# Staging of weight chunks: two steps ahead and in four buffers, with the low words converted in one piece

## The chip, the cores and the metric

The kernel runs on one NeuronCore of one Trainium2 chip. The metric is the device time of one execution in microseconds (us). Three runs of the kernel before took 1066.29, 1068.15 and 1068.39 us; the median is 1068.15.

## The reference, cut to what matters

Windowed attention with global tokens, then a feed-forward block. Batch 8, 8 heads, 512 local and 32 global tokens, head size 64; 4608 tokens in all, model width 512, inner width 2048.

```
s_ll = where(|i - j| <= 32, scale * q_l @ k_l^T, -1e9);  s_lg = scale * q_l @ k_g^T
out_l = softmax([s_lg, s_ll]) @ [v_g, v_l]
out_g = softmax(scale * q_g @ [k_g, k_l]^T) @ [v_g, v_l]
x = concat(out_g, out_l), heads side by side          # 4608 x 512
h = x @ w_in;  g = s * relu(h)**2 + b;  out = g @ w_out
```

The two weight matrices reach the kernel as 64-bit floats (they are passed as 64-bit words, two 32-bit words each). The kernel itself turns every value into a pair of 32-bit numbers, a rounded high part and a rest, with which TensorE later multiplies.

## The kernel before

The work is a sequence of steps j = 0, 1, 2, ... (the loop at the end of the function). Step j holds one attention slot (128 slots: batch, half of the 512 tokens, head) and, from step 10 on, one piece m = j - 10 of the feed-forward block (FFN; 136 pieces: 17 token tiles by 8 pairs of weight rows). Slot names carry their number: `sm9` is the softmax tile of slot 9, `ps_s9` its scores, `ps_t9` its transposed weights, `ps_o9` the products with the values, `rq9` and `rk9` its loaded queries and keys, `rv9` its values. FFN piece m has `ps_h` (first product), `r` (relu and square), `g` and the accumulators `acc`.

Slots 0 to 15 work with full 32-bit multiplication, slots from 16 on with split numbers: `kq` holds the split keys and queries of two slots, `vs` split values, `vsg` and `pg` what the global tokens need. `xs` (two buffers) holds the split tokens of a tile: tile 0 is complete after slot 7, tile 1 after slot 15.

The weights come in 16 chunks. Chunk k is 128 rows of `w_in` and 128 of `w_out`, two loads of 512 KB into a staging tile `wst`. Its decoding (`weight_words`) goes back and forth between ScalarE (ACT) and VectorE (DVE):

- ACT L155: the low words, converted (`wup`), 512 at a time, in the two buffers of `vs`
- ACT L157: the high words, scaled, over the low words
- DVE L158: shift and mask; DVE L162: add `wup`; DVE L163: put the sign back
- ACT L168: the high part into `w_all`; DVE L169: the rest into `w_all`

FFN piece m multiplies with chunks 2m and 2m + 1 (for m = 0 to 7; later tiles use the same weights). Chunks 0 and 1 are staged in the two `xs` buffers, chunks 2 to 15 in the two buffers of `kq`. Step j issues the loads of chunk j and then its decoding, so that a load must wait until the chunk two before it has been decoded.

The order of instructions on each engine isn't the program's order: the tile framework lists the instructions by a simulated time line, with priorities from the program's order. Each engine then works through its list in order; SyncE's queue (SP) issues nearly all loads, in order too, and waits where a buffer isn't free. For the first ten slots some matmuls on a constant tile (`warm`, L104) keep TensorE (PE) busy.

Of the kernel before, what the change touches and what calls it, by code (L numbers as in the profile page):

```python
# [11 lines left out]
F32R = mybir.dt.float32r  # L12
BF16 = mybir.dt.bfloat16
I32 = mybir.dt.int32
U32 = mybir.dt.uint32
U16 = mybir.dt.uint16
I16 = mybir.dt.int16
AF = mybir.ActivationFunctionType
ALU = mybir.AluOpType
# [3 lines left out]
P = 128  # L23
HALF = 256
# [7 lines left out]
NC = 416  # L32
# [19 lines left out]
WARM_FIRST = 28  # L52
WARM_HEAD = 4

SPOTS = ["xs"] * 2 + ["kq"] * 14
CHUNKS_AT = {j: 1 for j in range(16)}
BY_HALVES = 2
NORM_ACT = lambda j: j < NF
X_ACT = lambda j: j >= 8
# [2 lines left out]
G_LD = (0, 2)  # L62
G_PV = (1, 3)
GL_POOL = lambda m: False
XS_GAP, G_GAP = 0, 0
K_POOL = lambda j: j % 2


def f32(ap):
    return ap.bitcast(F32)  # L70
# [3 lines left out]
def window_attention_then_ffn(ctx: ExitStack, tc: tile.TileContext, qd, qg, kw, vw, vg, qz, qgz, vz, w_in, w_out, sv, bv, out):  # L74
    nc = tc.nc
    scale = 1.0 / math.sqrt(D)

    ops = ctx.enter_context(tc.tile_pool(name="ops", bufs=1))
# [1 line left out]
    masks = {first: ops.tile([P, 192 if first else 224], BF16, name=f"mask{int(first)}") for first in (True,)}  # L80
    w_all = ops.tile([P, 2, 16, 2, DM], F32R, name="w_all")
    gap = ops.tile([P, 240], F32, name="gap")
    for tag, n, bufs in (("vs", 512, 2), ("qgs", 512, 1), ("u", 256, 1), ("xs", 2048, 2), ("sm", NC, 2), ("pt", 2 * NC, 2), ("space", 16, 1), ("g", 1024, 2)):
        ops.tile([P, n], F32R, tag=tag, name=f"first_{tag}", bufs=bufs)
    const = ctx.enter_context(tc.tile_pool(name="const", bufs=1))
    sb = ctx.enter_context(tc.tile_pool(name="sb", bufs=2))
# [22 lines left out]
    for first, parts in ((True, ((32, 192, 0),)), (False, ((0, 160, 0), (192, 224, 32)))):  # L109
# [3 lines left out]
        for c0, c1, skip in parts:  # L113
            for sign, base in ((1, c0 - skip), (-1, 64 - c0 + skip)):
                nc.gpsimd.affine_select(
                    out=mask[:, c0:c1], in_=mask[:, c0:c1], pattern=[[sign, c1 - c0]], compare_op=ALU.is_ge,
# [11 lines left out]
    unread = sb.tile([P, 1], F32, tag="gm", name="unread", bufs=1)  # L128
    nc.scalar.activation(out=unread, in_=warm[:, 0:1], func=AF.Exp)

    def split_tile(tag, name, shape, gap):
        n = math.prod(shape)
        whole = ops.tile([P, n + gap], F32R, tag=tag, name=name, bufs=2)
        return whole[:, 0:n].rearrange("p (a b c) -> p a b c", a=shape[0], b=shape[1])

    def weight_chunk(k):
        st = ops.tile([P, 2048], I32, tag=SPOTS[k], name=f"wst{k}", bufs=2)
        n = 2 if k < BY_HALVES else 1
        sources = (w_in[k], w_out[k * P:(k + 1) * P, :])
        for i in range(2):  # L140
            queue = nc.scalar if k == 0 else nc.sync
            queue.dma_start(st[:, 1024 * i:1024 * (i + 1)], sources[i])
        for i in range(n):
            c = 1024 // n
            weight_words(k, st[:, 2 * c * i:2 * c * (i + 1)], slice(c * i, c * (i + 1)))

    def weight_words(k, st, at):
        words = st.rearrange("p (n w) -> p n w", w=2)
        low, high = words[:, :, 0], words[:, :, 1]
        n = at.stop - at.start  # L150
        parts = [slice(c, c + 512) for c in range(0, n, 512)]
        ups = []
        for h in parts:
            up = ops.tile([P, 512], I32, tag="vs", name=f"wup{k}_{at.start + h.start}", bufs=2)
            nc.scalar.activation(out=up, in_=low[:, h].bitcast(U32), func=AF.Copy, scale=2.0**-29)  # L155
            ups.append(up)
        nc.scalar.activation(out=low.bitcast(F32), in_=high.bitcast(F32), func=AF.Copy, scale=2.0**-112)  # L157
        nc.vector.tensor_scalar(  # L158
            out=low, in0=low, scalar1=3, scalar2=0x7FFFFFFF, op0=ALU.logical_shift_left, op1=ALU.bitwise_and,
        )  # L160
        for h, up in zip(parts, ups):
            nc.vector.tensor_tensor(out=low[:, h], in0=low[:, h], in1=up, op=ALU.add)  # L162
        nc.vector.scalar_tensor_tensor(  # L163
            out=high, in0=high, scalar=-2**31, in1=low, op0=ALU.bitwise_and, op1=ALU.bitwise_or,
        )
        m = high.bitcast(F32)
        hi, lo = (w_all[:, i, k].rearrange("p w c -> p (w c)")[:, at] for i in range(2))
        nc.scalar.copy(out=hi, in_=m)  # L168
        nc.vector.tensor_sub(out=lo, in0=m, in1=f32(hi))  # L169
# [190 lines left out]
    def qg_load(b):  # L360
        rqg = sb.tile([P, H * SG], F32, tag="xr", name=f"rqg{b}", bufs=1)
        nc.sync.dma_start(rqg, qgz[0] if b == 0 else qg[b])
        st_["rqg", b] = rqg

    def qg_load32(b):
        n = min(NF - 16 * b, H) * SG
        rqg = ops.tile([P, n], F32, tag="u", name=f"rqw{b}", bufs=1)
        nc.sync.dma_start(rqg, qgz[b, :, 0:n])
        st_["rqg", b] = rqg
# [129 lines left out]
    xs_ = {}  # L499

    def x_split(t):
        xs = split_tile("xs", f"xs{t}", [2, 4, HALF], XS_GAP)
        x = xcur.pop(t)
        for i in range(2):
            v = slice(2 * i, 2 * i + 2)
            nc.scalar.copy(out=xs[:, 0, v, :], in_=x[:, v, :])
            nc.vector.tensor_sub(out=xs[:, 1, v, :], in0=x[:, v, :], in1=f32(xs[:, 0, v, :]))
        xs_[t] = xs

    def xg_split(t):  # L510
        xs = split_tile("xs", f"xs{t}", [2, 4, HALF], XS_GAP)
        for i in range(2):
            xr = sb.tile([P, DM], F32, tag="r", name=f"xgr{i}", bufs=2)
            nc.sync.dma_start(xr, xg_d[i * P:(i + 1) * P, :])
            p_t = ps.tile([P, 4, P], F32, tag="t", name=f"ps_xg{i}")
            for c in range(4):
                nc.tensor.transpose(out=p_t[:, c, :], in_=xr[:, c * P:(c + 1) * P], identity=ident)
            q = slice(i * P, (i + 1) * P)
            nc.scalar.copy(out=xs[:, 0, :, q], in_=p_t)
            nc.vector.tensor_sub(out=xs[:, 1, :, q], in0=p_t, in1=f32(xs[:, 0, :, q]))  # L520
        xs_[t] = xs
# [3 lines left out]
    def ffn_in(m):  # L525
        t, pr = m // 8, m % 8
        xs = xs_[t]
        p_h = ps.tile([P, 2, HALF], F32, tag="h", name=f"ps_h{m}", bufs=2)
        for k in range(2):
            f = 2 * pr + k  # L530
            n = 0
            for c in range(4):
                for a, e in ((0, 0), (0, 1), (1, 0)):
                    nc.tensor.matmul(  # L534
                        p_h[:, k], lhsT=wi[:, a, f, c], rhs=xs[:, e, c, :],
                        start=(n == 0), stop=(n == 11),
                    )
                    n += 1
        r = sb.tile([P, 2, HALF], F32, tag="r", name=f"r{m}", bufs=2)
        nc.scalar.activation(out=r, in_=p_h, func=AF.Relu)  # L540
        nc.vector.scalar_tensor_tensor(out=r, in0=p_h, scalar=s_t, in1=r, op0=ALU.mult, op1=ALU.mult)  # L541
        g = split_tile("g", f"g{m}", [2, 2, HALF], G_GAP)
        if GL_POOL(m):
            nc.vector.tensor_scalar_add(r, r, b_t)
            nc.scalar.copy(out=g[:, 0], in_=r)
            nc.gpsimd.tensor_sub(out=g[:, 1], in0=r, in1=f32(g[:, 0]))
        else:
            nc.scalar.activation(out=g[:, 0], in_=r, func=AF.Identity, bias=b_t)  # L548
            nc.vector.scalar_tensor_tensor(  # L549
                out=g[:, 1], in0=r, scalar=b_t, in1=f32(g[:, 0]), op0=ALU.add, op1=ALU.subtract,  # L550
            )
        gs_[m] = g
# [35 lines left out]
    for b in range(B):  # L588
        for g in range(2):
# [4 lines left out]
            for i in range(2):  # L594
                h = 4 * g + 2 * i
# [19 lines left out]
    piece, last = 0, None  # L615
# [3 lines left out]
    for j in range(NM + LAG + 2):  # L619
        sp(j + 1)  # L620
        ld(j + 2)
        vl(j)
        for _ in range(CHUNKS_AT.get(j, 0)):
            weight_chunk(piece)
            piece += 1
        if j < NS:
            b1 = j // 16 + 1
            if j == 14 and NF > 16:
                qg_load32(1)
            elif j % 16 == 14 and b1 < B:  # L630
                qg_load(b1)
            sc(j)
            if j == NF - 1 and NF % 16:
                if NF > 16:
                    qg_load(j // 16)
                qg_split(j // 16)
            if j % 16 == 15 and NF <= j + 1 < NS:
                qg_split(b1)
        if j in early:
            early.pop(j)()  # L640
        m = j - LAG if LAG <= j < NM + LAG else None
        if m is not None:
            ffn_in(m)
            if m == 8 * 15 + 7:
                xg_split(16)
        tr(j - 1)
        transposes_and_pv(j - 1, j - 2)
        vsp(j - 1)
        for fn in extra.pop(j, []):
            fn()  # L650
        pvs(j - 2)
        vl32(j)
        if j in SPLIT_AT:
            x_split(SPLIT_AT[j])
        if last is not None:
            ffn_out(last)
        last = m
        if j in late:
            late.pop(j)()
# [79 lines left out]
```

## Time and profile before

| | us |
|---|---|
| median of three runs | 1068.15 |
| profiled execution | 1067.84 |
| its span | 1066.1 |
| PE busy / DVE / ACT / POOL in the span | 1024.1 / 814.6 / 725.6 / 315.0 |
| warm matmuls L104 | 18.6 |

PE is busy for 96% of the span, but not evenly: of 40 slices those after the sixth all show 9 (90% or more) except the last, and the first six show 9, 7, 8, 9, 7 and 7. "Busy" includes time at the lower clock and the warm matmuls. DMA is busiest in the same first slices.

### The profile page before, as it was taken

Reading aid. Unit: us, or ns where it says so; the run is one execution under the profiler, and the core shown is the slowest. Engines: PE = TensorE matmul, PEld = TensorE weight load, DVE = VectorE, ACT = ScalarE, POOL = GpSimd, SP = SyncE. Lnnn points to the kernel's source line nnn. Section 1 sums busy time; section 2 is a strip of 40 time slices with the busy share of each in tenths; the row PEclk is TensorE's granted clock in tenths of the full one; section 3 lists DMA queues with packets and bytes.
Section 4 is the critical chain, followed back from the end, with each engine's and each line's share of the span. In section 5 each row is a group of like instructions: output and inputs, shape, how many; then the busy total and the mean of one; then the engine's idle time right before and its main releaser. Section 6 shows DMA issues by size and latency. Waiting matters only on the chain.

```text
span 1066.1 us, 20403 instructions
## 1 busy us (share of the span) xinstructions
PE 1024.1 (96%) x7100; PEld 925.0 (87%) x7100; DVE 814.6 (76%) x2069; ACT 725.6 (68%) x1821; POOL 315.0 (30%) x365
## 2 busy tenths in 40 slices
PE   9789779999999999999999999999999999999996
PEld 4578669999999998999999999999999999999895
DVE  5878785887879968897879887997889787964321
ACT  6897685776768767786778676876678677743221
POOL 1000151432434423442344242432344234301000
PEclk9899789999999999999999999999999999999998
DMA  6755341221213222221323121322222122201000
GB/s 258 234 174 192 121 129 45 87 91 34 91 59 107 61 67 64 80 89 41 95 66 99 51 90 58 98 72 67 64 80 90 42 94 65 73 1 47 22 20 20
DMA packets 63535, 88.89 MB, mean 83 GB/s; under 512 B 7624, under 2 KB 48584, under 8 KB 63432
## 3 DMA queue, kind: packets, MB, share of 16 engines
q1 hardware_dynamic: 63144, 86.54, 25.9%
q8 instruction: 56, 0.92, 0.3%
q10 hardware_dynamic: 288, 1.05, 0.3%
q14 instruction: 47, 0.39, 0.1%
HBM read 78.12 MB, written 9.44 MB: 82 GB/s over the span
## 4 chain that ended last, share of the span: by engine, by line
PE 78%; DVE 8%; ACT 6%; DMA 5%; issue 1%; POOL 0%; SPq 0%; ACTq 0%; DVEq 0%; POOLq 0%
PE acc L566 32%; PE ps_h L534 30%; PE ps_t L326 4%; PE ps_o L412 4%; PE ps_s L385 4%; DMA wst<-in_w_in 2%; DMA wst<-in_w_out 2%; PE ps_og L486 2%; ACT sm L232 1%; DVE sm L242 1%; PE ps_g L391 1%; DVE w_all L169 1%; PE ps_tg L464 1%; DVE wst L162 1%; ACT wst L157 1%
## 5 line engine op out<-in xcount | busy, mean ns | idle before, releaser
L534 PE MATMUL ps_h<-xs,w_all 128*128 128x256 f32 x3264 | 441.0, 282 | 10.9 <-DVE w_all L169 3.9
L534 PEld LDWEIGHTS ps_h<-xs,w_all 128*128 128x128 f32 x3264 | 410.4, 190 | 22.9 <-DVE w_all L169 4.6
L566 PE MATMUL acc<-w_all,g 128*128 128x512 f32 x1632 | 426.1, 398 | 0.6 <-ACT g L548 0.3
L566 PEld LDWEIGHTS acc<-w_all,g 128*128 128x128 f32 x1632 | 291.5, 189 | 51.8 <-ACT g L548 1.1
L206 POOL TENSOR_TENSOR kq<-rq,kq 128x256 fp32r<-128x256 f32 x112 | 98.2, 877 | 235.8 <-ACT kq L205 219.8
L214 POOL TENSOR_TENSOR vs<-rv,vs 128x256 fp32r<-128x256 f32 x112 | 85.8, 766 | 261.4 <-ACT vs L213 248.5
L541 DVE SCALAR_TENSOR_TENSOR r<-ps_h,s_t,r 128x512 f32<-128x512 f32 x136 | 101.4, 746 | 61.2 <-ACT r L540 60.8
L540 ACT ACTIVATE r<-ps_h 128x512 f32<-128x512 f32 x136 | 81.1, 597 | 83.1 <-PE ps_h L534 75.5
L232 ACT ACTIVATE sm<-sm,nm 128x224 f32<-128x224 f32 (+1 forms) x256 | 118.5, 466 | 20.8 <-DVE nm L226 19.6
L549 DVE SCALAR_TENSOR_TENSOR g<-r,b_t,g 128x512 fp32r<-128x512 f32 x136 | 107.3, 789 | 32.6 <-ACT g L548 28.4
L548 ACT ACTIVATE g<-r,b_t 128x512 fp32r<-128x512 f32 x136 | 98.8, 727 | 45.8 <-DVE r L541 44.3
L226 DVE CUSTOM_DVE_ANT_0 sm<-ps_s,mask 128x224 f32<-128x224 f32 (+1 forms) x256 | 85.3, 368 | 23.4 <-PE ps_t L326 12.6
L326 PE MATMUL ps_t<-ident,sm 128*128 128x128 f32 x512 | 95.5, 280 | 5.1 <-ACT sm L240 5.0
L478 POOL TENSOR_TENSOR vsg<-rvg,vsg 128x320 fp32r<-128x320 f32 x64 | 57.1, 911 | 94.3 <-ACT vsg L477 94.2
L412 PE MATMUL ps_o<-pt,vs 128*128 128x256 f32 x448 | 83.6, 282 | 0.8 <-DVE u L424 0.8
L242 DVE TENSOR_SCALAR sm<-sm,nm 128x192 f32<-128x192 f32 (+1 forms) x224 | 81.8, 405 | 3.3
L385 PE MATMUL ps_s<-kq 128*128 128x192 f32 (+1 forms) x448 | 78.0, 280 | 4.3 <-ACT u L423 2.7
L385 PEld LDWEIGHTS ps_s<-kq 128*128 128x128 f32 x448 | 68.9, 193 | 10.6 <-ACT u L423 2.8
L395 ACT COPY tg<-ps_g 32x256 f32<-32x256 f32 (+1 forms) x112 | 42.2, 377 | 46.4 <-PE ps_g L391 44.0
L204 POOL TENSOR_TENSOR kq<-rk,kq 64x416 fp32r<-64x416 f32 x56 | 66.8, 1193 | 21.6 <-ACT kq L203 18.2
L401 ACT CAST pt<-ps_t 128x416 fp32r<-128x416 f32 x112 | 57.3, 511 | 22.9 <-PE ps_t L326 22.2
L412 PEld LDWEIGHTS ps_o<-pt,vs 128*128 128x128 f32 x448 | 67.1, 191 | 3.6 <-DVE u L424 1.0
(73 smaller groups left out, 1240.2 us busy)
## 6 DMA issues: line engine op xcount, KB each, us to landing
rq<-in_qd SPq DMA_DIRECT2D x112, 128.0 KB, 2.0
rv<-in_vw SPq DMA_DIRECT2D x112, 128.0 KB, 2.0
rk<-in_kw SPq DMA_DIRECT2D x64, 208.0 KB, 2.4
rvg<-in_vg SPq DMA_DIRECT2D x32, 320.0 KB, 2.9
out<-o SPq DMA_DIRECT2D x34, 256.0 KB, 2.2
wst<-in_w_in SPq DMA_DIRECT2D x15, 512.0 KB, 4.4
wst<-in_w_out SPq DMA_DIRECT2D x15, 512.0 KB, 5.5
rv<-in_vz SPq DMA_DIRECT2D x16, 256.0 KB, 3.0
```

The lines of the kernel that those rows point to most:

```text
L206: nc.gpsimd.tensor_sub(out=qs[:, 1, :], in0=rq, in1=f32(qs[:, 0, :]))
L214: nc.gpsimd.tensor_sub(out=vs[:, :, 1, :], in0=rv4, in1=f32(vs[:, :, 0, :]))
L232: nc.scalar.activation(out=p, in_=p, func=AF.Exp, bias=nm[:, blk:blk + 1], scale=-1.0, accum_out=ss[:, blk:blk + 1],)
L242: nc.vector.tensor_scalar(out=p, in0=p, scalar1=ss[:, blk:blk + 1], scalar2=1.0, op0=ALU.mult, op1=ALU.mult,)
L326: nc.tensor.transpose(out=p_t[:, at:at + P], in_=sm[:, c0:c0 + P], identity=ident)
L385: nc.tensor.matmul(p_s[:, cols], lhsT=qs[:, a, blk * P:(blk + 1) * P], rhs=ks[:, cols], start=(a == 0), stop=(a == 1),)
L412: nc.tensor.matmul(p_o[:, blk, :, q0:q0 + n], lhsT=vs[:, 2 * blk + c], rhs=pt[:, :, o], start=(c == 1), stop=(c == 0),)
L534: nc.tensor.matmul(p_h[:, k], lhsT=wi[:, a, f, c], rhs=xs[:, e, c, :], start=(n == 0), stop=(n == 11),)
L541: nc.vector.scalar_tensor_tensor(out=r, in0=p_h, scalar=s_t, in1=r, op0=ALU.mult, op1=ALU.mult)
L548: nc.scalar.activation(out=g[:, 0], in_=r, func=AF.Identity, bias=b_t)
L549: nc.vector.scalar_tensor_tensor(out=g[:, 1], in0=r, scalar=b_t, in1=f32(g[:, 0]), op0=ALU.add, op1=ALU.subtract,)
L566: nc.tensor.matmul(oacc[t][i], lhsT=g[:, a, k, i * P:(i + 1) * P], rhs=wo[:, e, f, :], start=(pr == 0 and n == 0), stop=(pr == 7 and n == 5),)
```

## The change

The staging tiles of the weights get four buffers in place of two. The two buffers of `xs` become two tags of one buffer each, `xs0` and `xs1` (even and odd token tiles), so that each can be named: chunk 4 is staged in `xs0` too, and chunks 5, 8, 11 and 14 in `xs1`; the rest stay in `kq`. The loads become a function of their own, `weight_load`, that step j calls for chunk j + 2 (steps 0 and 1 call it for four chunks), while `weight_chunk` decodes chunk j at step j as before. The low words of a chunk from 2 on are converted in one instruction of 1024 in place of two of 512, and added in one; `wup` moves from the `vs` buffers to those of `vsg` (even chunks) and `pg` (odd chunks). XS_GAP and G_GAP, which were 0, go.

```
-SPOTS = ["xs"] * 2 + ["kq"] * 14
-CHUNKS_AT = {j: 1 for j in range(16)}
+SPOTS = ["xs0", "xs1", "kq", "kq"] * 2 + ["xs1", "kq", "kq"] * 2 + ["xs1", "kq"]
+LOADS_AT = {0: (0, 1), 1: (2, 3), **{j: (j + 2,) for j in range(2, 14)}}
...
-    def weight_chunk(k):
-        st = ops.tile([P, 2048], I32, tag=SPOTS[k], name=f"wst{k}", bufs=2)
-        n = 2 if k < BY_HALVES else 1
+    staged = {}
+
+    def weight_load(k):
+        st = ops.tile([P, 2048], I32, tag=SPOTS[k], name=f"wst{k}", bufs=1 + (SPOTS[k] == "kq"))
+        staged[k] = st
         sources = (w_in[k], w_out[k * P:(k + 1) * P, :])
         for i in range(2):
             queue = nc.scalar if k == 0 else nc.sync
             queue.dma_start(st[:, 1024 * i:1024 * (i + 1)], sources[i])
+
+    def weight_chunk(k):
+        st = staged.pop(k)
+        n = 2 if k < BY_HALVES else 1
...
-        parts = [slice(c, c + 512) for c in range(0, n, 512)]
-        ups = []
-        for h in parts:
-            up = ops.tile([P, 512], I32, tag="vs", name=f"wup{k}_{at.start + h.start}", bufs=2)
-            nc.scalar.activation(out=up, in_=low[:, h].bitcast(U32), func=AF.Copy, scale=2.0**-29)
-            ups.append(up)
+        pool, tag = ((ops, "vsg"), (sb, "pg"))[(k + at.start // 512) % 2]
+        up = pool.tile([P, n], I32, tag=tag, name=f"wup{k}_{at.start}", bufs=1)
+        nc.scalar.activation(out=up, in_=low.bitcast(U32), func=AF.Copy, scale=2.0**-29)
...
-        for h, up in zip(parts, ups):
-            nc.vector.tensor_tensor(out=low[:, h], in0=low[:, h], in1=up, op=ALU.add)
+        nc.vector.tensor_tensor(out=low, in0=low, in1=up, op=ALU.add)
...
-        for _ in range(CHUNKS_AT.get(j, 0)):
-            weight_chunk(piece)
+        for k in LOADS_AT.get(j, ()):
+            weight_load(k)
+        if j < 16:
+            weight_chunk(j)
             piece += 1
```

How the order of instructions moves is shown at three places. The first is SP's queue of loads, around those of chunk 8 (`wst8`), in the kernel before (a name's last number is a buffer's):

```order
L276 DMA rq13_725<-in_qz 128x256
L270 DMA rk14_821<-in_kw 128x416
L281 DMA rv10_723<-in_vz 128x512
L362 DMA rqg1_1022<-in_qg 128x256
L276 DMA rq14_823<-in_qz 128x256
L281 DMA rv11_805<-in_vz 128x512
L142 DMA wst8_553<-in_w_in 128x1024
L142 DMA wst8_553<-in_w_out 128x1024
L142 DMA wst9_595<-in_w_in 128x1024
L142 DMA wst9_595<-in_w_out 128x1024
```

The same place of SP's queue in the changed kernel:

```order
L271 DMA rk8_444<-in_kw 128x416
L277 DMA rq8_446<-in_qz 128x256
L143 DMA wst8_448<-in_w_in 128x1024
L143 DMA wst8_448<-in_w_out 128x1024
L282 DMA rv5_442<-in_vz 128x512
L282 DMA rv6_483<-in_vz 128x512
L143 DMA wst9_487<-in_w_in 128x1024
L143 DMA wst9_487<-in_w_out 128x1024
L277 DMA rq9_485<-in_qz 128x256
```

The loads of chunk 8 stood behind the queries of slot 14 and now stand behind those of slot 8.

The second place is ACT's list just ahead of the relu of FFN piece 3 (`r3`), in the kernel before:

```order
L155 ACTIVATE wup9_0_598<-wst9_595 128x512
L155 ACTIVATE wup9_512_600<-wst9_595 128x512
L548 ACTIVATE g2_880<-r2_877,b_t_87 128x512
L157 ACTIVATE wst9_595<-wst9_595 128x1024
L168 CAST w_all_60<-wst8_553 128x1024
L240 ACTIVATE sm13_924<-sm13_924,nm13_925 128x224
L240 ACTIVATE sm13_924<-sm13_924,nm13_925 128x192
L540 ACTIVATE r3_960<-ps_h3_935 128x512
```

ACT's list ahead of the same relu in the changed kernel:

```order
L158 ACTIVATE wup15_0_1060<-wst15_879 128x1024
L549 ACTIVATE g2_854<-r2_851,b_t_88 128x512
L233 ACTIVATE sm13_895,nm13_896<-sm13_895,nm13_896 128x224
L233 ACTIVATE sm13_895,nm13_896<-sm13_895,nm13_896 128x192
L241 ACTIVATE sm12_816<-sm12_816,nm12_817 128x224
L241 ACTIVATE sm12_816<-sm12_816,nm12_817 128x192
L204 CAST kq16_1053<-rk16_975 64x416
L204 CAST kq16_1053<-rk16_975 64x416
L159 ACTIVATE wst15_879<-wst15_879 128x1024
L478 CAST vsg0_0_1227<-rvg0_0_1225 128x5x64
L478 CAST vsg0_0_1227<-rvg0_0_1225 128x5x64
L541 ACTIVATE r3_931<-ps_h3_906 128x512
```

At the same relu the decoding stood at chunk 9 and now stands at chunk 15, while attention stands at slot 13 in both.

The third place is PE's list just ahead of the first product of FFN piece 9 (`ps_h9`), in the kernel before:

```order
L391 MATMUL ps_g20_1644<-kq20_1518,qgs1_1125 64x256
L385 MATMUL ps_s21_1732<-kq20_1518 128x192 x2
L385 MATMUL ps_s21_1732<-kq20_1518 128x224 x2
L326 MATMUL ps_t19_1694<-ident_58,sm19_1534 128x128 x4
L412 MATMUL ps_o18_1691<-pt18_1592,vs18_1595 128x256
L412 MATMUL ps_o18_1691<-pt18_1592,vs18_1595 128x2x64
L412 MATMUL ps_o18_1691<-pt18_1592,vs18_1595 128x256
L412 MATMUL ps_o18_1691<-pt18_1592,vs18_1595 128x2x96
L385 MATMUL ps_s22_1844<-kq22_1723 128x192 x2
L385 MATMUL ps_s22_1844<-kq22_1723 128x224 x2
L534 MATMUL ps_h9_1547<-xs1_1387,w_all_60 128x256 x24
```

PE's list ahead of the same product in the changed kernel:

```order
L413 MATMUL ps_o16_1424<-pt16_1313,vs16_1316 128x2x64
L327 MATMUL ps_t17_1427<-ident_58,sm17_1264 128x128 x2
L413 MATMUL ps_o16_1424<-pt16_1313,vs16_1316 128x256
L413 MATMUL ps_o16_1424<-pt16_1313,vs16_1316 128x2x96
L327 MATMUL ps_t17_1427<-ident_58,sm17_1264 128x128 x2
L567 MATMUL acc0_1_785<-w_all_60,g7_1305 128x512 x5
L392 MATMUL ps_g18_1378<-kq18_1248,qgs1_1084 64x256
L567 MATMUL acc0_1_785<-w_all_60,g7_1305 128x512
L386 MATMUL ps_s19_1486<-kq18_1248 128x192 x2
L386 MATMUL ps_s19_1486<-kq18_1248 128x224 x2
L535 MATMUL ps_h9_1506<-xst1_1346,w_all_60 128x256 x24
```

At this product attention had come to the scores of slot 22 and now comes to those of slot 19; the second product (`acc`) of piece 7 now stands ahead of it.

## Rows read from the trace of the kernel before

**Rows 1.** Two stretches: start:end, length, busy us and count by engine, granted clock, DMA.
```profile
0.00:160.00 160.00, 130.40 (x727) 101.81 (x728) 121.99 (x281) 126.23 (x282) 24.68 (x36) 0.89 0.54 184
160.00:1066.10 906.10, 893.66 (x6374) 823.17 (x6374) 692.64 (x1789) 599.34 (x1541) 290.30 (x329) 1.00 0.22 66
```
**Rows 2.** Chain that ended last, first 160 us: shares by line.
```profile
by line: DMA wst<-in_w_in 16.5%; DMA wst<-in_w_out 11.1%; DVE w_all L169 7.1%; DVE wst L162 5.5%; ACT wst L157 5.3%; ACT wup L155 4.6%; issue 4.4%; ACT w_all L168 4.4%; ACT sm L232 3.7%; PE ps_o L350 2.3%; DVE wst L158 2.2%; DVE wst L163 2.
```
**Rows 3.** Waits of SP's queue, first 160 us: total us, times, longest.
```profile
SPq L142 <- DVE w_all L169: 32.5, 7, 8.7
```
**Rows 4.** Waits of ACT, first 160 us.
```profile
ACT w_all L168 <- DVE wst L163: 12.4, 7, 3.5
ACT wup L155 <- DMA wst<-in_w_in: 10.0, 7, 3.3
```
**Rows 5.** Waits of PE, first 160 us.
```profile
PE ps_h L534 <- DVE w_all L169: 3.9, 3, 1.7
PE ps_h L534 <- ACT w_all L168: 3.7, 3, 2.1
```
**Rows 6.** Decoding by line, first 160 us: count, busy us, mean ns, idle before.
```profile
L162 DVE CUSTOM_DVE_ANT_0 wst<-wst,wup 128x1024 uint16<-128x1024 uint16 x32 | 23.4, 768 | 0.3
L155 ACT ACTIVATE wup<-wst 128x512 int32<-128x512 uint32 x32 | 21.4, 673 | 14.4 <-DMA wst<-in_w_in 10.0 <-DVE wst L162 1.5 <-DVE r L541 1.4
L169 DVE TENSOR_TENSOR w_all<-wst,w_all 128x1024 fp32r<-128x1024 f32 x14 | 17.8, 1270 | 4.9 <-ACT w_all L168 4.8
...
L157 ACT ACTIVATE wst<-wst 128x1024 f32<-128x1024 f32 x14 | 15.9, 1135 | 0.0
L168 ACT CAST w_all<-wst 128x1024 fp32r<-128x1024 f32 x14 | 15.9, 1134 | 12.4 <-DVE wst L163 12.4
...
L158 DVE TENSOR_SCALAR wst<-wst 128x1024 int32<-128x1024 int32 x14 | 9.7, 695 | 4.9 <-ACT wst L157 4.0 <-DMA rq<-in_qz 0.7
```
**Rows 7.** ACT up to the relu of FFN piece 3, and from there to 159.89.
```profile
6.00:86.27 80.27, 70.46 (x164) 0.94 0.65 225
86.27:159.89 73.62, 54.13 (x117) 0.84 0.45 147
```
**Rows 8.** DVE from its first decoding to its part of that relu.
```profile
7.36:88.84 81.48, 65.12 (x161) 0.94 0.63 216
```
**Rows 9.** ACT in order of time: start, us, line, tile, shape.
```profile
39.19 1.12 ACT L157 ACTIVATE wst<-wst 128x1024 f32<-128x1024 f32 x1
40.21 0.81 ACT L240 ACTIVATE sm<-sm,nm 128x192 f32<-128x192 f32 x2
...
86.27 0.59 ACT L540 ACTIVATE r<-ps_h 128x512 f32<-128x512 f32 x1
```
**Rows 10.** PE in order of time.
```profile
97.10 0.86 PE L292 MATMUL ps_s<-rk,rq 128*128 128x224 f32 x4
97.80 1.94 PE L350 MATMUL ps_o<-pt,rv 128*128 128x128 f32 x16
...
130.26 2.07 PE L566 MATMUL acc<-w_all,g 128*128 128x512 f32 x4
...
159.89 4.68 PE L534 MATMUL ps_h<-xs,w_all 128*128 128x256 f32 x39 [0.25 <-DVE r L541]
164.42 1.08 PE L566 MATMUL acc<-w_all,g 128*128 128x512 f32 x4
...
168.24 0.60 PE L464 MATMUL ps_tg<-ident,sg 128*128 128x128 f32 x4
168.59 0.68 PE L412 MATMUL ps_o<-pt,vs 128*128 128x256 f32 x4
169.11 2.93 PE L566 MATMUL acc<-w_all,g 128*128 128x512 f32 x12
171.88 0.60 PE L326 MATMUL ps_t<-ident,sm 128*128 128x128 f32 x4
```
**Rows 11.** Loads of a chunk: line, queue, count, KB each, us to landing.
```profile
wst<-in_w_in SPq DMA_DIRECT2D x15, 512.0 KB, 4.4
wst<-in_w_out SPq DMA_DIRECT2D x15, 512.0 KB, 5.5
```
**Rows 12.** PE in 20 us: busy us, granted clock.
```profile
120.00:140.00 20.00, 16.42 (x85) 0.66 0.38 130
```

More of the change, by code (lines that the diff above doesn't have):

```diff
@@ L64 @@
 GL_POOL = lambda m: False
-XS_GAP, G_GAP = 0, 0
 K_POOL = lambda j: j % 2
@@ L82, in window_attention_then_ffn @@
     gap = ops.tile([P, 240], F32, name="gap")
-    for tag, n, bufs in (("vs", 512, 2), ("qgs", 512, 1), ("u", 256, 1), ("xs", 2048, 2), ("sm", NC, 2), ("pt", 2 * NC, 2), ("space", 16, 1), ("g", 1024, 2)):
+    for tag, n, bufs in (("vs", 512, 2), ("qgs", 512, 1), ("u", 256, 1), ("xs0", 2048, 1), ("xs1", 2048, 1), ("sm", NC, 2), ("pt", 2 * NC, 2), ("space", 16, 1), ("g", 1024, 2)):
         ops.tile([P, n], F32R, tag=tag, name=f"first_{tag}", bufs=bufs)
@@ L129, in window_attention_then_ffn, with split_tile @@
     nc.scalar.activation(out=unread, in_=warm[:, 0:1], func=AF.Exp)
-    def split_tile(tag, name, shape, gap):
+    def split_tile(tag, name, shape, bufs):
         n = math.prod(shape)
-        whole = ops.tile([P, n + gap], F32R, tag=tag, name=name, bufs=2)
+        whole = ops.tile([P, n], F32R, tag=tag, name=name, bufs=bufs)
         return whole[:, 0:n].rearrange("p (a b c) -> p a b c", a=shape[0], b=shape[1])
-    def weight_chunk(k):
-        st = ops.tile([P, 2048], I32, tag=SPOTS[k], name=f"wst{k}", bufs=2)
-        n = 2 if k < BY_HALVES else 1
+    staged = {}
+    def weight_load(k):
+        st = ops.tile([P, 2048], I32, tag=SPOTS[k], name=f"wst{k}", bufs=1 + (SPOTS[k] == "kq"))
+        staged[k] = st
         sources = (w_in[k], w_out[k * P:(k + 1) * P, :])
@@ L501, in x_split @@
     def x_split(t):
-        xs = split_tile("xs", f"xs{t}", [2, 4, HALF], XS_GAP)
+        xs = split_tile(f"xs{t % 2}", f"xst{t}", [2, 4, HALF], 1)
         x = xcur.pop(t)
@@ L510, in xg_split @@
     def xg_split(t):
-        xs = split_tile("xs", f"xs{t}", [2, 4, HALF], XS_GAP)
+        xs = split_tile(f"xs{t % 2}", f"xst{t}", [2, 4, HALF], 1)
         for i in range(2):
@@ L541, in ffn_in @@
         nc.vector.scalar_tensor_tensor(out=r, in0=p_h, scalar=s_t, in1=r, op0=ALU.mult, op1=ALU.mult)
-        g = split_tile("g", f"g{m}", [2, 2, HALF], G_GAP)
+        g = split_tile("g", f"g{m}", [2, 2, HALF], 2)
         if GL_POOL(m):
```

## The prediction

> **What bounds the kernel now.** I read the windows of the span first, then the chain that ended last, the waits by engine, the decoding line by line, and ACT, DVE and PE in order of time.
>
> The windows cut the kernel in two [rows 1]. From 160 us on, PE is busy for 893.66 of 906.10 us at a granted clock of 1.00: there it is the bound, and nothing that ACT, DVE or a load does faster helps. In the first 160 us it is busy for 130.40, part of that warm matmuls and part at the lower clock (0.89 in the mean), while ACT has 126.23 us of work and DVE 121.99: no engine is full. So the change can only act by bringing PE earlier to the state that it has at 160 us. As a mark I take the start of `ps_h9`, at 159.89 [rows 10].
>
> What fills the first stage is the chain of the weights: loads of `wst` are 27.6% of the chain that ended last in it, lines of the decoding another third [rows 2]. SP waits 32.5 us in seven times with a staging load until the last instruction of an earlier chunk (L169) has freed the buffer [rows 3]; ACT waits for landings (10.0 us) and, within the decoding, for DVE (12.4 us) [rows 4]; PE waits for finished weights, 3.9 and 3.7 us [rows 5].
>
> **The change part by part.**
>
> *Loads.* With four buffers and the loads ahead in SP's list, a load waits for the chunk four before it, not two. A load takes 4.4 to 5.5 us from issue to landing [rows 11]; three chunks of decoding in between last longer. By the order, chunk 8's loads now stand behind the queries of slot 8, not of slot 14. Of ACT's 10.0 us, 3.3 is chunk 0's load at the start, which stays, as does about 1.6 of chunk 1's; I take 3 us as the part that goes ahead of the relu of piece 3 (below). A few chunks (6 and 11 by the order) have a load right behind a query load that waits for PE; that can leave 2 to 3 us twice. Ends: 0 and 5 gained; I take 3.
>
> *One conversion for two.* A 512 conversion lasts 673 ns; one of 1024 isn't in the trace, and the nearest row is L157 with the same elements, 1135 [rows 6]. ACT's instructions overlap: L157 lasts 1.12 but the next starts 1.02 later [rows 9]. So two of 0.57 become one of 1.03: 0.11 us for each of 14 chunks, 1.5 us. DVE's add: 692 ns typical, so two of about 0.60 become one like L169 (1.22, 1.14 with the overlap): under 0.1 us each, 1 us. Ends: 0 to 2.5; I take 1.5 on either engine. It is in the sums below. Against it: the one conversion needs both halves of the chunk, and the second lands later, 5.5 against 4.4 us from an issue some 0.4 later [rows 11]; for a chunk that is late this is 1.5 us more, for one on time nothing.
>
> The Trainium skill ("Perfetto Trace Analysis", section "Optimizing Scalar/DVE Operations") says that where ScalarE or VectorE isn't saturated but makes others wait, instructions cut in pieces may let work finish sooner; that speaks against the merge. By it, 14 late chunks would lose 21 us; by the rows ACT is 88% busy in the stretch at issue [rows 7], so I hold it for nearly saturated and the rule for not binding; the trace of before has no merged conversion to show it.
>
> *New waits.* `wup` now shares buffers with `vsg` and `pg`, so the first `vsg` conversions move from early in ACT's list to behind chunk 14, and SP holds the next load of that tile, with the keys and queries of slots 17 to 20 behind it, until POOL is done. PE then has FFN pieces 3 to 7 ready, which cover it; without that cover 0 to 3 us. I take 0.
>
> *The order.* This is the largest term. ACT's list now holds the decoding of all chunks up to `wup15` ahead of the relu of piece 3 (`r3`), where it held chunks up to 9. Counted in the two lists up to `r3`: conversions of low words 20 of 512 become 4 of 512 and 14 of 1024 (+5.3 us), L157 gains 6 (+6.2), L168 gains 5 (+5.2), two key conversions come (+0.9), two normalisations go (-0.7). ACT's work up to there was 70.5 of 80.27 us [rows 7]; it becomes 70.5 + 16.9, about 87. DVE: L158 +6 (3.6), adds +6.2, L163 and L169 +5 each at 1.14 (11.4), one key (0.5): 65.1 of 81.48 [rows 8] becomes about 87. Both engines now carry the same 87 us up to `r3`.
>
> How long do 87 us take? ACT was busy for 88% of its stretch [rows 7]; without the 3 us of landings that would be 91%. DVE was at 80% [rows 8] and must rise. I take 89%: `r3` starts at 6.0 + 87/0.89 = 104 (before: 86.27). Ends: 94% gives 98.6, 80% gives 115.
>
> *From there PE.* All weights are then there or nearly so, and PE has only to work its list. In the new order, from the end of piece 3's `ps_h` to `ps_h9`: 120 `ps_h` at 4.53/39 = 0.116 (13.9 us), 72 `acc` at 2.77/12 = 0.231 (16.6 us), three pairs of value products at 1.94, two full-precision scores at 0.70, and some fourteen groups of four at 0.35 to 0.52 (13.2 us together) [rows 10]: 44 us. If PE has by then also done piece 4's `ps_h`, which the two `ps_h` buffers allow, 35. I take 40, and 3 for stalls and clock: `ps_h9` starts at 104 + 43 = 147. By the same count ACT has 28 and DVE 25 us of work in these 43, so they are not the bound.
>
> At `ps_h9` the old order had done three slots of scores, two of transposes and values and one global piece more (3.9 us), the new one 12 `acc` more (2.8): the new one owes 1.1 us. From there on the kernels are alike: 906.2 us to the span's end, and 1.7 around it.
>
> **The sum:** 159.89 - 147 - 1.1 = 11.8 us less. The profiled execution (1067.84) would become 1056.0; the median of 1068.15 is 0.3 above it, so 1056.3, rounded 1056. In general the time is 1068.15 + (start of `r3`) - 115.8.
>
> **The rivals.** I count as no change what lies within 0.2% (2.1 us), which is about what a measurement of this kernel can tell.
>
> - *The wait moves from landings to the ACT-DVE chain, and the gain is lost.* With all chunks decoded ahead of `r3`, DVE carries 33% more there. If it stays at its 80%, `r3` comes at 115 and the time is 1067. For it: the longest of ACT's waits are already for DVE [rows 4]. Against: part of these waits followed from late landings, since a late `wup` delays all behind it. Chance 0.08, with the case that SP's list still keeps the loads late.
> - *Slower.* The decoding of chunks 10 to 15 displaces attention and keeps PE from its first FFN products; both engines idle as ACT did after 86 us, 54.13 of 73.62 or 74% [rows 7]. `r3` then starts at 6 + 87/0.74 = 124 and the time is 1076. It decides from an `r3` later than 118. For it: in the new order piece 0 can start only behind 12 chunks' work; against: in that stretch of before the loads of chunks 10 to 15 came late, which is what goes. Chance 0.09.
> - *The clock.* Where PE had gaps it was granted less: 0.66 from 120 to 140 us, and four `acc` took 2.07 us there against 1.08 at full clock [rows 10, 12]; these are the levels of 1.2 and 2.4 GHz. PE has less to do before `r3` now. If as much of 20 us were lost behind `r3`, that is 0.34 x 20 = 6.8 us, 4 more than my 3, and the time is 1060 (1063 if the 3 were all other stalls). The Trainium skill ("TensorE: Matmul & The Clock Gate", section "HAM oscillation") says that a PE which waits between bursts is throttled again and starts each burst slowly; the trace agrees, with the 0.66. Behind `r3` PE has its list full, as after 160 us, where the clock was 1.00 [rows 1]. Chance 0.13.
> - *More.* ACT and DVE at 94%, PE through piece 4 by `r3` and no stalls: `r3` at 98.6, `ps_h9` at 134: 1043. Chance 0.10.
>
> **How the numbers follow.** The forecast has the remaining 0.60, with 1050 to 1062 for itself. Faster: 0.60 + 0.13 + 0.10 = 0.83; same 0.08; slower 0.09. The range reaches from 1046 (most of the case with more) to 1067 (the lost gain); above and below it lie about 2 in 10.
>
> **What would show it.** In the changed profile: SP's waits of staging loads for L169 gone or short; ACT's waits for `wst` landings down to those of chunks 0 and 1; the decoding at its end by about 110 us; `r3` at 104, after the 86 of before; `ps_h9` at about 147; PE at 9 in the slices after that, with the same 906 us to the end. It is wrong if `r3` starts later than 115, if PE waits for weights behind `r3`, or if the stretch behind `ps_h9` isn't 906 us.

## The result and the profile after

The changed kernel takes 1048.24 us (median of four runs, 1047.48 to 1049.18), the kernel before 1067.22 (four runs, 1065.94 to 1068.39): ratio 0.9823 with a 95% interval of 0.9805 to 0.9840. The forecast of 1056 had the direction, and the time lies inside its range, but the gain is 19 us and not 12. The profiled execution took 1049.18 us, its span 1047.4.

First the windows of the changed kernel, in the columns of [rows 1]: the same cut at 160 us, then the stretches up to the relu of FFN piece 3 (`r3`) and from there to the first product of piece 9 (`ps_h9`).

```profile
0.00:160.00 160.00, 138.85 (x840) 112.19 (x841) 127.14 (x282) 131.78 (x283) 26.68 (x38) 0.93 0.56 190
160.00:1047.40 887.40, 875.48 (x6262) 806.77 (x6260) 683.74 (x1773) 592.01 (x1526) 287.66 (x327) 1.00 0.22 66
0.00:102.65 102.65, 81.50 (x422) 58.96 (x423) 84.01 (x176) 89.21 (x174) 4.95 (x17) 0.88 0.70 245
102.65:141.44 38.79, 38.79 (x278) 35.78 (x278) 28.47 (x65) 29.58 (x74) 15.71 (x15) 1.00 0.29 84
```

PE does 840 matmuls in the first 160 us where it did 727; behind them the kernels are alike. The fourth line is where the time comes from: from `r3` to `ps_h9` PE is busy without a gap, at a clock of 1.00. These are the two marks, on ACT and on PE:

```profile
102.65 0.60 ACT L541 ACTIVATE r<-ps_h 128x512 f32<-128x512 f32 x1
...
141.44 3.00 PE L535 MATMUL ps_h<-xst,w_all 128*128 128x256 f32 x24
```

Up to `r3` the change costs 102.65 - 86.27 = 16.4 us [rows 9]. From `r3` to `ps_h9` it takes 38.79 us in place of 73.62 [rows 7, 10], which gives back 34.8. The rest, from `ps_h9` to the end of the span, is 1047.40 - 141.44 = 906.0, before 906.2. What PE has done more by 160 us is read from the groups of its first 160 us (count, busy us, mean ns). The kernel before:

```profile
L534 PE MATMUL ps_h<-xs,w_all 128*128 128x256 f32 x217 | 34.4, 305 | 8.9 <-DVE w_all L169 3.9 <-ACT w_all L168 3.7 <-DVE r L541 1.4
L566 PE MATMUL acc<-w_all,g 128*128 128x512 f32 x84 | 25.7, 440 | 0.6 <-ACT g L548 0.3
```

The changed kernel:

```profile
L535 PE MATMUL ps_h<-xst,w_all 128*128 128x256 f32 x288 | 40.6, 289 | 0.1
L567 PE MATMUL acc<-w_all,g 128*128 128x512 f32 x122 | 33.6, 403 | 0.0
```

71 first products and 38 second ones more, at the 0.116 and 0.231 us of the prediction, are 8.2 + 8.8 = 17.0 of the 18.7 us by which the spans differ. The means fell too (305 to 289, 440 to 403 ns), and the granted clock of these 160 us rose from 0.89 to 0.93: more of them ran at the higher level.

PE's whole span says how the 18.7 us divide, the kernel before first, then the changed one:

```profile
PE 1024.1 (96%) x7100; PEld 925.0 (87%) x7100; DVE 814.6 (76%) x2069; ACT 725.6 (68%) x1821; POOL 315.0 (30%) x365
PE 1014.3 (97%) x7100; PEld 919.0 (88%) x7100; DVE 810.9 (77%) x2055; ACT 723.8 (69%) x1807; POOL 314.3 (30%) x365
```

The same 7100 matmuls are busy for 9.8 us less, and PE stands idle for 33.1 us in place of 42.0. So about half of the gain is idle time of PE that was filled, and the other half is time that the same matmuls took less. The second half goes with the higher clock; no run holds the clock fixed, to show that it is all clock.

The waits of the first 160 us (total us, times, longest), in the changed kernel, SP's queue first, then ACT:

```profile
SPq L282 <- PE ps_o L351: 31.1, 12, 6.9
SPq L143 <- DVE w_all L170: 13.5, 6, 4.1
...
ACT wup L158 <- DMA wst<-in_w_out: 5.6, 4, 2.3
ACT wup L158 <- DMA wst<-in_w_in: 5.1, 2, 3.5
...
PE ps_g L301 <- DMA rk<-in_kw: 4.0, 5, 2.1
```

SP's wait of staging loads for the last instruction of a decoding fell from 32.5 to 13.5 us [rows 3]; PE's waits for finished weights [rows 5] are gone. SP waits more for PE to be done with older values instead (`rv`, L282: 31.1 us, before 16.7). But ACT still waits 10.7 us for weights to land, as before [rows 4]: what went there is its 12.4 us for DVE ahead of the cast of the high part, now 0.2, in the second line below. The decoding by line, up to 140 us (count, busy us, mean ns, idle before) on ACT and DVE:

```profile
L158 ACT ACTIVATE wup<-wst 128x1024 int32<-128x1024 uint32 x14 | 16.3, 1162 | 4.9 <-DMA wst<-in_w_out 4.9
L169 ACT CAST w_all<-wst 128x1024 fp32r<-128x1024 f32 x14 | 16.4, 1173 | 0.2 <-DVE wst L164 0.2
...
L163 DVE CUSTOM_DVE_ANT_0 wst<-wst,wup 128x2048 uint16<-128x2048 uint16 x14 | 17.7, 1263 | 0.1
```

The 1024 conversion lasts 1162 ns, where the prediction went by a row of 1135. Its 4.9 us of waits are for `w_out`, the half that lands later: in the kernel before, ACT's conversions waited for that half once, for 0.9 us.

### The profile page after: what moved, and what is told of

Same layout as the page of the kernel before. It is cut to its first block, busy times and chain, and to the rows that moved or that the text cites. A ratio compares the mean times of both kernels' runs of the same rounds, so it can differ in the third digit from the quotient of the medians.

```text
span 1047.4 us, 20372 instructions
## 1 busy us (share of the span) xinstructions
PE 1014.3 (97%) x7100; PEld 919.0 (88%) x7100; DVE 810.9 (77%) x2055; ACT 723.8 (69%) x1807; POOL 314.3 (30%) x365
## 4 chain that ended last, share of the span: by engine, by line
PE 83%; DVE 7%; ACT 4%; DMA 3%; issue 1%; SPq 0%; POOL 0%; DVEq 0%; ACTq 0%; POOLq 0%
PE acc L567 35%; PE ps_h L535 32%; PE ps_t L327 4%; PE ps_o L413 4%; PE ps_s L386 4%; PE ps_og L487 2%; DMA rk<-in_kw 1%; PE ps_g L392 1%; DVE sm L243 1%; DMA wst<-in_w_in 1%; PE ps_tg L465 1%; ACT sm L233 1%; DVE r L542 1%; PE ps_o L351 1%; DVE sm L227 1%
## 5 line engine op out<-in xcount | busy, mean ns | idle before, releaser
L535 PE MATMUL ps_h<-xst,w_all 128*128 128x256 f32 x3264 | 437.9, 281 | 2.0 <-DVE r L542 1.0
L535 PEld LDWEIGHTS ps_h<-xst,w_all 128*128 128x128 f32 x3264 | 408.2, 189 | 12.1 <-DVE r L542 2.4
```

What stands on the lines that cost most here:

```text
L535: nc.tensor.matmul(p_h[:, k], lhsT=wi[:, a, f, c], rhs=xs[:, e, c, :], start=(n == 0), stop=(n == 11),)
```

## The experiments

The gain could come from any of four parts: the buffers, the loads two steps ahead (the lead), the merged conversion, or the order of instructions that the scheduler makes of them. Theory A is the prediction's: loads that no longer wait for a decoding let ACT and DVE do all decoding earlier. B gives the gain to the merge, C to the lead; D holds that landings of loads bound the stage and not the work of ACT and DVE.

**The merge alone**, in the kernel before:

```
-            up = ops.tile([P, 512], I32, tag="vs", ..., bufs=2)          (two of 512)
+        up = pool.tile([P, n], I32, tag=tag, ..., bufs=1)                (one of 1024)
```

> The kernel before with only the low words converted and added 1024 at a time (wup in the buffers of vsg and pg); two staging buffers, loads as before. Theory A (the two staging buffers hold the decoding back; the merge saves 1.5 us on ACT and 1 on DVE): 1065, at least 1060, SP still waiting some 30 us for L169 of an earlier chunk. Rival B (the merge and the freed vs buffers carry the gain): 1055 or less.

Measured: 1070.73 us, ratio 1.0030 (1.0018 to 1.0041). B falls, and so does A's size: the kernel is 3 us slower here. ACT's waits in the first 160 us, then SP's for a free staging buffer:

```profile
ACT wup L153 <- DMA wst<-in_w_out: 17.4, 10, 6.5
ACT w_all L164 <- DVE wst L159: 6.8, 4, 3.4
...
SPq L142 <- DVE w_all L165: 10.5, 5, 3.4
```

The merged conversion can start only when both halves of a chunk are there: 17.4 us in ten waits, where 0.9 us were spent before. A is wrong on SP, too: its wait for a free staging buffer is 10.5 us and not some 30. SP waits longer for PE's scores (31.7 us, before 14.0) and for POOL's keys (23.5, before 16.4) instead, and PE waits 9.6 us for loaded keys (before 1.5). Which of these waits carries the 3 us no run isolates. The prediction held the rule of the Trainium skill ("Perfetto Trace Analysis", "Optimizing Scalar/DVE Operations"), that cut instructions may let work finish sooner, for not binding. With two buffers the trace agrees with its direction; the 21 us that the prediction put on it were far too many.

**The rest without the merge**, in the changed kernel (two conversions of 512, in `vs`, again):

> The changed kernel with the low words converted as before, 512 at a time in the buffers of vs; four staging buffers and loads two steps ahead stay. Theory A (the buffers carry the gain): 1050, the 2 us being the merge. Rival B (the merge carries it): 1060 or more.

Measured: 1048.39 us, 0.9818 (0.9801 to 0.9835). The changed kernel had 0.9823: with four buffers the merge neither costs nor gives, so A's 2 us for it are not there.

**No lead**, in the changed kernel:

```
-LOADS_AT = {0: (0, 1), 1: (2, 3), **{j: (j + 2,) for j in range(2, 14)}}
+LOADS_AT = {j: (j,) for j in range(16)}
```

> The changed kernel with the loads of chunk j called in step j, as before; four staging buffers and the merge stay. Theory A (the number of buffers lets the scheduler place the loads early, the two steps add little): 1049, within 3 us of the changed kernel. Rival C (the two steps' lead carries the gain): 1057 or more, with ACT waiting 10 us more for landings.

Measured: 1044.74 us, 0.9783 (0.9767 to 0.9799). C falls, and A's "within 3 us" is missed as well: the lead does not help, it costs about 3.5 us.

**Three steps ahead**, in the changed kernel:

> The changed kernel with the loads called three steps ahead (chunks 0 to 3 in step 0, chunk j + 3 in step j). Leaving the lead out gave 1044.7, two steps 1048.2. Theory E (each step of lead puts staging loads in front of attention's on SP and lets decoding displace attention): 1050 or more. Rival F (a lead shortens the waits of ACT for landings, 10.7 us with two steps): 1045 or less.

Measured: 1050.58 us, 0.9844 (0.9827 to 0.9862). E's time came and F's did not. So 0, 2 and 3 steps give 1044.7, 1048.2 and 1050.6; the intervals of 0 and 2 steps are apart, those of 2 and 3 overlap. The Trainium skill ("DMA: Bandwidth & Descriptors", "Rules for kernel authors") advises to issue a transfer early and to wait for it late. Here an earlier issue did not help. A load issued earlier also stands ahead of others in SP's queue, of the keys that PE needs among them. PE's waits for loaded keys (`ps_g` for `rk`) add up to 4.0 us with two steps, 6.0 with three and 0.8 with none. A load of keys landed 2.8 us after its issue in the kernel before and 5.6 us in the changed one, in the first 160 us of each:

```profile
rk<-in_kw SPq DMA_DIRECT2D x14, 208.0 KB, 2.8
```

```profile
rk<-in_kw SPq DMA_DIRECT2D x14, 208.0 KB, 5.6
```

That the keys carry the price of the lead is not shown. Their landing time does not follow the lead: it is 5.4 us with three steps and 4.6 without lead, and with the 512 conversions 3.5 us with two steps and 4.4 without.

**The buffers alone**: neither lead nor merge.

> The changed kernel with four buffers, the loads in their own step and the low words converted 512 at a time: of the change only the buffers are left. Theory A (the buffers carry the gain, merge and lead add nothing): 1044 to 1047. Rival (merge and no lead only work together): 1050 or more.

Measured: 1045.75 us, 0.9798 (0.9780 to 0.9816). With and without lead and merge, the four combinations with four buffers lie between 1044.7 and 1048.4, the two with two buffers at 1067 and 1071 (a lead with two buffers wasn't run). The buffers carry the gain. With the 512 conversions the lead costs 2.6 us, by intervals that overlap.

**Three buffers** from chunk 2 on, no lead, 512 conversions:

```
+SPOTS = ["xs0", "xs1"] + ["kq", "kq", "xs1"] * 4 + ["kq", "kq"]
```

> The kernel before with three staging buffers from chunk 2 on (kq, kq, xs1 in turn), loads in their own step, 512 conversions: the kernel with four buffers, no lead and 512 conversions took 1045.75 us, the one with two took 1067.2. Theory I (the third buffer already breaks the chain of one load, one decoding, and the fourth helps only chunk 4): 1045 to 1049, SP's waits of staging loads for L169 near the 13.5 us of the changed kernel, relu of piece 3 at 92 to 96 us. Theory J (each buffer brings its share): about 1056, SP's waits for L169 above 20 us.

Measured: 1050.65 us, 0.9842 (0.9825 to 0.9858), between the two and nearer I, though I's marks are missed too (`r3` at 97.67; SP's wait 7.1 us). The third buffer brings some 17 us, and the version with four (which stages only chunk 4 in `xs0`, so that from chunk 8 on it has three as well) 5 more. Most later chunks also change places between `kq` and `xs1` between these two, so the 5 us are not shown to be the fourth buffer's alone. SP's wait of staging loads for the end of a decoding is 7.1 us here and 18.8 with four buffers, though that version is the faster one: this wait by itself doesn't rank the versions.

**A third buffer for the last chunks only**: the kernel before, with chunks 13 and 15 in `xs1`.

> The kernel before, two buffers for chunks 2 to 12, but chunks 13 and 15 staged in the second xs buffer, so that the last chunk does not share a buffer with the split keys of slots 16 and 17. Theory A (two buffers throughout are the cost): 1061 or more. Rival H (the loss is that chunk 15 comes only behind slot 17, and piece 7 with it): 1053 or less.

Measured: 1064.89 us, 0.9977 (0.9967 to 0.9987). The time is A's. But the run says little of H: the last cast of a high part comes at 145.99 us, only 2.6 us earlier than the 148.56 of the kernel before, so the chunk on which H puts the loss is still late. The run with late chunks, below, puts most of the gain at that chunk, as H had it.

**The staging loads on POOL's queue**, in the kernel before:

```
-            queue = nc.scalar if k == 0 else nc.sync
+            queue = nc.scalar if k == 0 else nc.gpsimd
```

> The kernel before with the staging loads of chunks 1 to 15 issued by POOL's queue in place of SP's; two staging buffers, 512 at a time. Theory A (two buffers hold the decoding back, whichever queue issues): 1062 or more. Rival G (SP's list, in which a staging load waits behind attention's loads, holds it): 1055 or less. If POOL's loads land later than 5 us, it is slower than before.

Measured: 1075.82 us, 1.0082 (1.0063 to 1.0101). G falls: away from SP's list the loads wait for their buffers all the same. The wait moves to POOL's queue, and grows from 32.5 us to 61.9; first POOL's wait, then what SP waits for behind it:

```profile
POOL wst L142 <- DVE w_all L169: 61.9, 7, 16.2
...
SPq L185 <- POOL kq L206: 27.2, 5, 22.2
```

A load that waits for its buffer stops POOL's own work on keys, and SP's next loads wait for that: 27.2 us, before 16.4. The landing is not the cause. The loads took 4.0 and 4.8 us from issue, on SP's queue 4.4 and 5.5 [rows 11].

**More work for ACT**: the low words of chunks 2 to 15 converted twice, 14 times some 1.03 us, in the changed kernel.

> The changed kernel with the conversion of the low words done twice for chunks 2 to 15 (14 more instructions of about 1.03 us on ACT, 12 or 13 of them ahead of the relu of piece 3). Theory A (the work of ACT and DVE sets when that relu comes, and PE from there on): the relu 10 to 13 us later, 1059 to 1061. Rival D (landings bound the stage, ACT still waits 10.7 us for them): the additional work fits into these waits, 1052 or less.

Measured: 1062.50 us, 0.9955 (0.9942 to 0.9967): 14.3 us more than the changed kernel by the medians, of a price of 14.4; the spans of the profiled executions differ by 12.1. D falls, but A's mark is missed: `r3` moves by 6 us, from 102.65 to 108.80, and not by 10 to 13. The last cast of a high part moves by 13, from 107.4 to 120.6. ACT's waits for landings fall from 10.7 to 7.1 us, and from 6.00 us up to `r3` it is now 96% busy (98.67 of 102.80 us). In the changed kernel the work of ACT up to the end of the decoding sets the time. More work for DVE wasn't tried.

**Order or loads?** Four buffers change two things: a load waits less, and the scheduler, which knows it, puts the decoding of the last chunks ahead of attention. Two runs try to take these apart. In the first, the kernel with the buffers alone calls chunks 4 to 15 two steps later, loads and decoding together:

```
+LOADS_AT = {0: (0,), 1: (1,), 2: (2,), 3: (3,), **{k + 2: (k,) for k in range(4, 16)}}
         for k in LOADS_AT.get(j, ()):
             weight_load(k)
-        if j < 16:
-            weight_chunk(j)
+            weight_chunk(k)
```

> Four buffers, 512 conversions, loads in the step of their decoding, but loads and decoding of chunks 4 to 15 called two steps later than in the kernel that took 1045.75 us. On ACT's list the same chunks stand ahead of the relus of pieces 0 to 3; chunk 15 now stands behind slot 19 where it stood ahead of slot 17, and piece 7's relu behind slot 20 as in the kernel before. Theory K (the extra buffers act through the order: the scheduler puts the last chunks ahead of attention, so that PE has FFN pieces early): 1055 to 1062, relu of piece 7 later than 140 us. Theory L (they act by letting a load run beside two decodings, wherever the chunk stands): 1045 to 1050, relu of piece 7 at 125 to 130 us.

Measured: 1059.82 us, 0.9927 (0.9904 to 0.9951): K's time. ACT waits 7.5 us for landings, with the buffers alone 4.5, so landings account for little of it. Up to `r6` the two run alike (118.08 against 116.03 us), but then chunk 15 is decoded at 139.6 us and not at 118.7, and `r7` starts at 145.81 in place of 125.15. The windows show PE short of work there; first the kernel with late chunks, then the one with the buffers alone:

```profile
120.00:140.00 20.00, 13.25 (x91) 11.39 (x89) 14.69 (x42) 13.21 (x34) 5.04 (x5) 0.91 0.31 96
140.00:160.00 20.00, 16.50 (x106) 15.33 (x107) 13.77 (x33) 12.02 (x31) 8.88 (x10) 0.83 0.34 100
```

```profile
120.00:140.00 20.00, 20.00 (x156) 18.91 (x155) 17.06 (x43) 16.09 (x43) 9.38 (x11) 1.00 0.37 111
140.00:160.00 20.00, 20.00 (x146) 18.41 (x145) 15.78 (x41) 13.03 (x34) 6.95 (x8) 1.00 0.26 77
```

The kernel before has the same hole, three slices long:

```profile
100.00:120.00 20.00, 14.91 (x79) 12.38 (x79) 15.77 (x26) 14.75 (x28) 0.00 (x0) 0.91 0.45 144
120.00:140.00 20.00, 16.42 (x85) 14.05 (x86) 13.80 (x32) 13.30 (x29) 5.04 (x5) 0.66 0.38 130
140.00:160.00 20.00, 12.32 (x81) 10.77 (x80) 18.96 (x48) 16.48 (x44) 13.56 (x15) 0.83 0.41 120
```

In the second run the kernel before, with its two buffers, is asked for an earlier decoding:

```
+            with tc.high_priority(offset=300):
                 weight_chunk(piece)
```

> The kernel before, two buffers, with the decoding given a higher priority: the loads of chunks 4 and 5 stand behind the queries of slot 4, where they stood behind those of slots 6 and 7, those of chunks 6 to 9 one to two slots earlier; chunks 10 to 15 stay. Theory K (order): the early relus come earlier but chunk 15 stands where it stood: 1062 to 1068. Theory L (two buffers hold each load until a decoding two before it ends): 1066 to 1070, SP's waits of staging loads for L169 at 30 us or more.

Measured: 1071.20 us, 1.0041 (1.0027 to 1.0056), above both ranges. The early relus come later, not earlier (`r0` at 76.27, before 70.07), and the last cast of a high part at 149.27 (148.56). SP's wait for L169 is 25.2 us, where L had 30 or more and the kernel before has 32.5. With two buffers the higher priority doesn't bring the end of the decoding forward; in SP's list it moved only the loads of chunks 4 to 9, so it leaves open what an earlier place of the last ones would do.

So about 14 of the 22 us between the kernel before and the buffers alone hang on when the last chunks are decoded, and of the versions run only those with more buffers for all chunks brought that forward by much. The other 8 remain with late chunks too; they are put down to the loads by what is left over, not by a run of their own.

One mark orders the versions in the rough: the start of the relu of piece 8 (`r8`), the first piece of the second token tile, behind the decoding of all chunks:

| version | r8 (us) | span (us) | difference |
|---|---|---|---|
| buffers alone | 134.63 | 1041.8 | 907.2 |
| no lead | 134.73 | 1042.7 | 908.0 |
| changed kernel | 138.85 | 1047.4 | 908.6 |
| three buffers | 139.79 | 1048.6 | 908.8 |
| three steps ahead | 140.64 | 1049.3 | 908.7 |
| the rest without the merge | 142.36 | 1047.5 | 905.1 |
| late chunks | 146.30 | 1058.0 | 911.7 |
| more work for ACT | 147.82 | 1059.5 | 911.7 |
| third buffer for the last chunks | 156.67 | 1063.4 | 906.7 |
| higher priority | 157.35 | 1069.4 | 912.1 |
| before | 157.98 | 1066.1 | 908.1 |
| merge alone | 162.66 | 1071.0 | 908.3 |
| POOL's queue | 163.44 | 1075.7 | 912.3 |

The mark spreads over 29 us, the difference over 7, between 905.1 and 912.3. So it tells the groups apart, but not neighbours: without the merge `r8` comes 3.5 us later than in the changed kernel, at the same span.

No version beats the two without lead: 1044.74 with the merge, 1045.75 without, their intervals overlapping. By the medians both beat the changed kernel, by 2.5 to 3.5 us; only the interval of the one with the merge is clear of it.

## Why the prediction was right, and where it was off

*The order.* It was called the largest term, and it is. ACT carries 87.7 us of work up to `r3` (87 forecast), DVE 84.3 (87):

```profile
6.00:102.65 96.65, 87.73 (x172) 0.88 0.73 254
...
7.36:103.50 96.14, 84.34 (x176) 0.88 0.72 251
```

ACT is 91% busy in its stretch and DVE 88%, where 89% was taken, so `r3` came at 102.65 and not at 104: 1.35 us.

*From `r3` on.* This is the mis-sized term: 40 us of work and 3 of stalls and clock were taken; measured were 38.79 with neither stall nor lower clock. That is 4.2 us. Of the counted products 118 of 120 first ones and 65 of 72 second ones fell into it. The debt of 1.1 us at `ps_h9` did not show either: 906.0 us follow, where 906.2 + 1.1 were counted, 1.3 us. 1.35 + 4.2 + 1.3 is 6.9 of the 6.8 us by which the profiled execution (1049.18) stands below 1056.0; the time around the span is 0.1 longer. The median is 0.9 lower still.

*Loads.* The 3 us of landing waits that were to go did not: 10.7 us stay. The lead, counted as a help, costs 3.5 us. And 4.9 of the 10.7 us are the merged conversion's waits for its second half: with the 512 ones all landing waits are 6.8 us, and without lead as well 4.5, of which 3.5 is one wait at the first chunk. SP's waits for a decoding did not go either, as the prediction's signs had it: 13.5 us of 32.5 stay. What went is the 12.4 us for DVE [rows 4], which the prediction did not price. It took a busy share of 89% for ACT, and 91% came by another wait than the one it named; as far as this share goes, it was luck. That the scheduler now has other chunks' work to put between a chunk's DVE part and its cast would explain it, but no run isolates this.

*The merge.* 1.5 us on ACT forecast; with four buffers the runs with and without differ by 0.2 (lead) and 1.0 us (no lead), in its favour and inside their intervals. With two buffers it costs 3. The instruction's duration was nearly right (1162 ns for 1135); that it is worth its duration was not.

*New waits.* SP held for `rvg` was taken at 0, and no run isolates it: PE shows no gap behind `r3`.

*The rivals.* The ACT-DVE chain did not keep its idle time (0.2 us ahead of the cast). The slower case, deciding from an `r3` later than 118, did not come near. The clock did fall, but ahead of `r3`, where ACT's work sets the time; these are PE's windows of the kernel before, and then of the changed one:

```profile
20.00:40.00 20.00, 15.43 (x79) 0.91 0.60 193
...
60.00:80.00 20.00, 17.82 (x129) 0.99 0.47 151
```

```profile
20.00:40.00 20.00, 16.51 (x75) 0.79 0.81 286
...
60.00:80.00 20.00, 13.04 (x62) 0.77 0.57 185
```

Behind `r3` it is 1.00, as the prediction argued from a full list. The Trainium skill says that a PE which waits between bursts is throttled ("TensorE: Matmul & The Clock Gate", "HAM oscillation"). Two stretches of the changed kernel agree: 13.04 busy of 20 us at 0.77, 38.79 of 38.79 at 1.00. The busy share by itself does not tell the clock, though: from 20 to 40 us PE is busier than before (16.51 us against 15.43) and has less of it (0.79 against 0.91). The hole of the kernel before, with its 0.66, is gone: there PE is now busy throughout, at 1.00.

What the formula for the time missed: it set the time by `r3`. The buffers alone have `r3` at 91.27 and no lead at 96.56, and the same time within 1 us; the three-buffer kernel has 97.67 and 1050.65. The formula rests on the prediction's sentence that behind `r3` all weights are there or nearly so. Where the last chunks come late it fails: the run with late chunks has `r3` at 90.36, which would give 1042.7, and took 1059.82. The later mark `r8`, behind the last weights, holds within some 7 us over all versions.

## What to carry to other kernels

Where a start-up stage decodes data that a saturated engine will need, look for the moment from which that engine never runs dry, and price a change by what it does to that moment: here 16 us later at an early mark still meant 19 us sooner at the end. When a pair of staging buffers ties every load to a decoding, try a third buffer first; here another queue and a higher priority with two buffers cost time, and so did a longer lead with four. Merging two instructions also merges their waits: here that came with 3 us more where two buffers held the loads back, and with no change of time where four did not.

## What was not expected

A lead of two or three steps on loads of 512 KB cost 3.5 and 5.8 us, though the buffers were there for it. Up to `r3` the weights and attention's loads share the DMA engines, at a mean busy share of 0.73 and 254 GB/s from 6 us on, where it was 0.65 and 225 [rows 7]; what is brought early there is brought ahead of something else. That this is the price of the lead is argued, not shown.
